# Loads of three weight matrices, one per head or half, with read descriptors over four partitions' rows, in a batched GQA decode kernel

## The chip, the cores and the metric

One core of one Trainium2 chip. The metric is the device time of one execution in microseconds (us), the median of several runs.

## The reference

```python
# B=4, one new token, D=448, 16 query heads, 8 KV heads, Sk=8192, Dh=256, bf16
xn = layernorm(A_x)
q  = xn @ A_wq                                   # (4, 16, 256)
p  = softmax(q @ k_cache.T * 256**-0.5)          # per head, over 8192 positions
s  = (p @ v_cache) @ A_wo                        # A_wo: 4096 x 448
g  = silu(mlp_block(xn))                         # small: B_w3 448 x 1792, B_w4 1792 x 448
out = A_x + s * g
# (layer norms, the unused token shift and B_w1, B_w2 left out)
```

The K and V caches are 268 MB of the 279 MB that must be read. The arithmetic is small beside that.

## The kernel before

SyncE issues all large loads on one queue. There are 32 (batch, KV head) pairs, called heads below. K and V each have two buffers of 32 KB per partition, and a load of 4 MB fills one: 128 rows of 32,768 B. `wq`, `w3` and `w4` lie in the V buffers at the start; `wo` has its own buffer.

```python
kn = sb("kn", [P, 2, NCH, DH], BF16)          # first buffer of the kernel
vb = sb("vb", [P, 2, NCH, DH], BF16)
kT = sb("kT", [P, RING, TB * P], BF16)
wo_sb = sb("wo_sb", [P, HQ, NHALF, D], BF16)
...
def prog_sp(sp):
    sp.dma_start(vflat[1][:, 0:DK * HDH], ... A_wq ...).then_inc(S["dwq"], 16)
    sp.dma_start(vflat[0][:, 0:DK * FH], ... B_w3 ...).then_inc(S["dw3"], 16)
    sp.dma_start(w4_sb..., B_w4.rearrange("(a p k) n -> p a (k n)", a=NHF, k=NFK)
                 ).then_inc(S["dw4"], 16)
    ...
    load_k(0)
    load_k(1)
    wo_src = A_wo.rearrange("(h p c) n -> p h (c n)", p=P, c=NHALF)

    def load_wo(lo, hi, sem):
        sp.dma_start(wo_sb[:, lo:hi].rearrange("p h c n -> p h (c n)"),
                     wo_src[:, lo:hi]).then_inc(S[sem], 16)

    load_wo(NLATE, HQ, "dwo")                 # heads 4..15, one load
    for h in range(2, NH):
        load_k(h)                             # waits until K buffer h % 2 is free
        load_v(h - 2)
    load_v(NH - 2)
    load_v(NH - 1)                            # in four pieces
    for i, hs in enumerate(LATE):             # heads (0, 1), (2,), (3,)
        load_wo(hs[0], hs[-1] + 1, "dwl%d" % i)
```

A partition holds, of each head of `wo`, two matrix rows that are adjacent in memory: 1,792 B. For one head the 128 partitions' pieces follow each other in memory, so 229 KB of source are contiguous, and the load takes them as 128 rows, one for each partition (the trace has 2,048 packets of 1,792 B for the 16 heads). For `w3` such a row is 12,544 B, for each half of `w4` 6,272 B.

TensorE transposes K (the lines `pst<-ident_b,kn`), multiplies with q, then multiplies the probabilities with V; VectorE and ScalarE move the transposes out of PSUM. At the end (`finish`) it works off the last heads and multiplies with `wo`.

Of the kernel before, what the change touches and what calls it, by code (L numbers as in the profile page):

```python
# [1 line left out]

# [10 lines left out]
P = 128  # L13
# [19 lines left out]
def bass_recurrent_scan__gqa_block_cached__mixer_s_mlp__decode_kernel(  # L33
# [16 lines left out]
    HQ = HD // DH  # L50
# [3 lines left out]
    NHF = 2  # L54
    DK = D * NHF // P
    assert D * NHF == DK * P and DK % 2 == 1 and D == DK * (P // 2)
    HDH, FH = HD // NHF, F // NHF
    NFK = FH // P
# [30 lines left out]
    LATE = ((0, 1), (2,), (3,))  # L89
    NLATE = sum(len(g) for g in LATE)  # L90
# [11 lines left out]
    with ExitStack() as es:  # L102
        def sb(name, shape, dty):
# [5 lines left out]
        wo_sb = sb("wo_sb", [P, HQ, NHALF, D], BF16)  # L109
# [46 lines left out]
        S = {n: es.enter_context(nc.semaphore(n)) for n in (  # L156
            ["dx", "dwq", "dw3", "dw4", "dwo", "dk0", "dk1", "dv0", "dv1", "dout"]
            + ["dvl%d" % i for i in range(NPIECE)] + ["dwl%d" % i for i in range(len(LATE))]
            + ["p_td", "p_ta", "p_sc", "p_m1", "p_m2", "p_m3", "p_tr", "p_ou", "p_pv", "p_x", "p_q", "p_h", "p_h2", "p_o"]
            + ["v_ev", "a_ev", "v_rmax", "v_diag", "v_neg", "v_ot", "a_exp", "g_q", "g_c",  # L160
               "v_s", "v_a", "v_qb", "p_qt", "v_h2", "p_hs", "v_k", "v_v", "v_po", "v_o", "g_o", "g_p", "g_f", "v_xT", "v_qT", "v_hT", "v_c", "v_w", "a_c", "v_out"])}


        vflat = [vb[:, i].rearrange("p c d -> p (c d)") for i in range(2)]
        wq_sb = vflat[1][:, 0:DK * HDH].rearrange("p (j n) -> p j n", j=DK)
        w3_sb = vflat[0][:, 0:DK * FH].rearrange("p (j n) -> p j n", j=DK)
        w4_sb = vflat[0][:, DK * FH:DK * FH + NF * D].rearrange("p (a k n) -> p a k n", a=NHF,
                                                                k=NFK)
# [16 lines left out]
        def store(eng, i):  # L185
            eng.dma_start(out2d[:, i * DQ:(i + 1) * DQ], out_b[i * PQ:i * PQ + Bn, :]
                          ).then_inc(S["dout"], 16)

        def prog_sp(sp):
            sp.dma_start(vflat[1][:, 0:DK * HDH],  # L190
                         A_wq.rearrange("d (t n) -> (d t) n", t=NHF).rearrange(
                             "(p j) n -> p (j n)", j=DK)).then_inc(S["dwq"], 16)
            sp.dma_start(vflat[0][:, 0:DK * FH],
                         B_w3.rearrange("d (t n) -> (d t) n", t=NHF).rearrange(
                             "(p j) n -> p (j n)", j=DK)).then_inc(S["dw3"], 16)
            sp.dma_start(w4_sb.rearrange("p a k n -> p a (k n)"),
                         B_w4.rearrange("(a p k) n -> p a (k n)", a=NHF, k=NFK)
                         ).then_inc(S["dw4"], 16)

            def load_k(h):  # L200
                b, g = where(h)
                if h >= 2:
                    sp.wait_ge(S["v_k"], h - 1)
                sp.dma_start(kn_dst(h), A_k_cache[b, g].rearrange("(p c) d -> p (c d)", p=P)
                             ).then_inc(S["dk%d" % (h % 2)], 16)

            def load_v(h):
                b, g = where(h)
                src = A_v_cache[b, g].rearrange("(p c) d -> p c d", p=P)
                if h < NH - 1:  # L210
                    sp.wait_ge(S["v_v"], h + 1)
                    sp.dma_start(vflat[h % 2], src.rearrange("p c d -> p (c d)")
                                 ).then_inc(S["dv%d" % (h % 2)], 16)
                else:

                    sp.wait_ge(S["v_k"], h)
                    for i in range(NPIECE):
                        lo, hi = PIECES[i], PIECES[i + 1]
                        sp.dma_start(
                            kn[:, 1 - h % 2, lo:hi, :].rearrange("p c d -> p (c d)"),  # L220
                            src[:, lo:hi, :].rearrange("p c d -> p (c d)")
                        ).then_inc(S["dvl%d" % i], 16)

            load_k(0)
            load_k(1)
            wo_src = A_wo.rearrange("(h p c) n -> p h (c n)", p=P, c=NHALF)

            def load_wo(lo, hi, sem):
                sp.dma_start(wo_sb[:, lo:hi].rearrange("p h c n -> p h (c n)"),
                             wo_src[:, lo:hi]).then_inc(S[sem], 16)  # L230

            load_wo(NLATE, HQ, "dwo")
            for h in range(2, NH):
                load_k(h)
                load_v(h - 2)
            load_v(NH - 2)
            load_v(NH - 1)
            for i, hs in enumerate(LATE):
                load_wo(hs[0], hs[-1] + 1, "dwl%d" % i)
            sp.wait_ge(S["v_out"], 1)  # L240
            store(sp, 0)
            take(sp, "dout", 16 * NDG)

        def take(eng, name, n=1):
            eng.wait_ge(S[name], n).then_inc(S[name], -n)  # L245
# [285 lines left out]
        def prog_pe(pe, xn_mark, xn2_mark):  # L531
            pe.wait_ge(S["g_c"], NPI)
            for k, (src, mark) in enumerate(((xn_b, xn_mark), (xn2_b, xn2_mark))):
                pe.wait_ge(S["v_c"], mark)
                for j in range(DK):
                    ins = pe.transpose(xT_ps[:, k, j, :],  # L536
                                       src[:, j].rearrange("b m t -> b (m t)"),
                                       ident_b[0:Bn, 0:Bn])
# [5 lines left out]
            for j in range(DK):  # L544
                for i in range(NQD):
                    ins = pe.matmul(q_ps[i * PQ:i * PQ + NHF * Bn, 0:QW],
                                    xnT[:, j].rearrange("p a b -> p (a b)"),
                                    wq_sb[:, j, i * QW:(i + 1) * QW],
                                    start=(j == 0), stop=(j == DK - 1))
# [4 lines left out]
            for k in range(NFK):  # L554
                for j in range(DK):
                    ins = pe.matmul(h_ps[:, k * NHF * Bn:(k + 1) * NHF * Bn], w3v[:, j, k, :],
                                    xn2T[:, j], start=(j == 0), stop=(j == DK - 1))
            ins.then_inc(S["p_h"], 1)
            take(pe, "v_qb")
            for m in range(QW // P):  # L560
                ins = pe.transpose(qt_ps[:, m * P:(m + 1) * P], q_b[:, m * P:(m + 1) * P],
                                   ident_b[:, :])
            ins.then_inc(S["p_qt"], 1)
            take(pe, "dw4", 16)
            take(pe, "v_hT")
            for k in range(NFK):
                for a in range(NHF):
                    i = k * NHF + a
# [5 lines left out]
            for i in range(NDG):  # L574
                ins = pe.matmul(hs_ps[i * PQ:(i + 1) * PQ, :], selb[:, :],
                                ou_f[:, i * DQ:(i + 1) * DQ], start=True, stop=True)
# [125 lines left out]

            def finish():
                f_bc(h)
                take(pe, "dwo", 16)
                pe.wait_ge(S["g_f"], 1)
                f_ou(range(NLATE, HQ - 3 * REP))
                take(pe, "v_po")
                f_warm(4)
                take(pe, "a_exp")  # L710
                pe.matmul(psm[:, P + REP:P + 2 * REP], ones_f[:, :], rowsum[:, h % 2, :],
                          start=True, stop=True)
                f_tr(ot_dst, REP).then_inc(S["p_m3"], 1)
                f_warm(2)
                take(pe, "dv%d" % ((h - 1) % 2), 16)
                f_pv(h - 1, 0, NCH)
                take(pe, "v_ot")
                f_ou(range(HQ - 3 * REP, HQ - 2 * REP))
                f_warm(2)
                take(pe, "v_po")  # L720
                f_tr(lambda dh: ot_dst(dh, 1), REP, 1).then_inc(S["p_tr"], 1)
                f_warm(3)
                take(pe, "dvl0", 16)
                pb = PIECES[NPIECE - ND]
                f_pv(h, 0, PIECES[1], pb, vl)
                take(pe, "v_ot")
                f_ou(range(HQ - 2 * REP, HQ - REP)).then_inc(S["p_ou"], 1)
                f_warm(3)
                for i in range(1, NPIECE - ND):
                    take(pe, "dvl%d" % i, 16)  # L730
                    f_pv(h, PIECES[i], PIECES[i + 1], pb, vl)
                take(pe, "v_a")
                for i in range(NDG):
                    pe.matmul(o_ps[i * PQ:(i + 1) * PQ, 0:DQ], selb[:, :],
                              ou_f[:, i * DQ:(i + 1) * DQ], start=True, stop=False)
                f_direct(NPIECE - ND)
                take(pe, "v_po")
                for dh in range(NHALF):
                    for i in range(CP):
                        pe.matmul(ol_ps[:, dh * PVW:(dh + 1) * PVW],  # L740
                                  po[:, 0, i * DH + dh:(i + 1) * DH:NHALF], sel[:, i, :],
                                  start=False, stop=False)
                f_direct(NPIECE - 1).then_inc(S["p_pv"], 1)
                take(pe, "dwl0", 16)
                f_o(LATE[0])
                take(pe, "v_ot")
                f_o(range(HQ - REP, HQ))
                for i in range(1, len(LATE)):
                    take(pe, "dwl%d" % i, 16)
                    ins = f_o(LATE[i], i == len(LATE) - 1)  # L750
                ins.then_inc(S["p_o"], 1)
# [61 lines left out]
```

## Time and profile before

| | before |
|---|---|
| median time | 657.61 us (657.61 to 658.30, 3 runs) |
| span of the profiled run | 656.9 us |
| DMA queue q1, share of 16 engines' span | 99.2% |
| TensorE busy | 85% |

These lines of the page of the kernel before say what bounds it. DMA is the busy share of the DMA engines in 40 slices of the span, in tenths; GB/s is what they moved.

```profile
DMA  8999999999999999999999999999999999999996
GB/s 360 440 413 425 434 427 437 425 439 427 437 427 435 429 435 431 431 435 427 437 429 433 429 433 429 433 429 433 429 435 431 433 431 435 429 433 433 429 425 256
DMA packets 12353, 279.13 MB, mean 425 GB/s; under 512 B 1204, under 2 KB 3256, under 8 KB 3768
...
q1 hardware_dynamic: 12328, 278.99, 99.2%
...
kn<-in_A_k_cache_dram SPq DMA_DIRECT2D x32, 4096.0 KB, 25.7
...
wo_sb<-in_A_wo_dram SPq DMA_DIRECT2D x1, 2688.0 KB, 44.3
```

The engines are at 9 tenths or more in every slice but the first and last. The third slice, where the first `wo` load runs, is at 413 GB/s, below its neighbours. A K load lands (its completion has arrived from all 16 DMA engines) 25.7 us after its issue though its bytes need 9.7 us (8 rows per engine at 1,213 ns): others stand ahead of it. The 2,052 packets between 512 B and 2 KB are the `wo` rows, and four others.

The stretch from 40 to 44 us lies inside the first `wo` load (the DMA view of the kernel before, that window):

```profile
DMA packets 855, 1.53 MB, mean 383 GB/s; under 512 B 0, under 2 KB 855, under 8 KB 855
```

The chain of waits of the kernel before, in order of time (start us, length us, what), is its last 3 us:

```profile
651.61 2.42 PE pst L687 x24
...
654.06 0.39 DVE res L526
...
654.47 0.38 DVE out_b L528
```

The 24 matmuls with the late `wo` start right after the first late `wo` load has landed on its slowest engine (651.48), so the chain runs back into the DMA stream.

The table of stretches of the kernel before; columns are stretch, length, busy us of PE, PEld, DVE, ACT and POOL with counts, granted TensorE clock, DMA share, GB/s:

```profile
620.00:624.00 4.00, 2.88 (x24) 2.70 (x25) 1.14 (x2) 0.90 (x1) 0.00 (x0) 0.62 0.99 426
624.00:628.00 4.00, 4.00 (x94) 4.00 (x92) 2.14 (x4) 3.02 (x8) 0.00 (x0) 0.95 0.97 418
```

TensorE has just begun the last head here, after a wait for its K, and the granted clock is below full for part of it. The clock records show one stretch at half clock of 3.4 us (621.0 to 624.4), and one from 651.7 us on, over the last 24 matmuls.

### The profile page before, as it was taken

What the parts mean: (1) busy time and instruction counts of PE and PEld (TensorE: products, weight loads), DVE (VectorE), ACT (ScalarE), POOL (GpSimd) and SP (SyncE); (2) the same over time, 40 slices, a digit from 0 to 9 for tenths busy, and PEclk for the clock granted to TensorE, in tenths of its full rate; (3) what the DMA queues carried; (4) which work ended last, traced back from release to release, by engine and by line L of the source; (5) the groups of instructions that cost most, each with busy time, mean ns of one, the idle gap of its engine ahead of it and who ended that gap; (6) DMA issues with size and microseconds to landing.
All of it is one profiled execution on the core that took longest, in us unless ns stands there. A gap on an engine that the chain in (4) does not pass through costs nothing. (4 is left out here: it accounts for less than half of the span.)

```text
span 656.9 us, 22864 instructions
## 1 busy us (share of the span) xinstructions
PE 556.3 (85%) x9937; PEld 476.3 (73%) x9937; DVE 276.5 (42%) x589; ACT 256.0 (39%) x364; POOL 13.4 (2%) x77
## 2 busy tenths in 40 slices
PE   1899997988888988888897888898888889888897
PEld 0487886876766887667787766798767678766775
DVE  7353554443443444434443443444334443433442
ACT  4144544442433443323444333444333344433340
POOL 2000000000000000000000000000000000000000
PEclk9698999887899878889987888988878987887998
DMA  8999999999999999999999999999999999999996
GB/s 360 440 413 425 434 427 437 425 439 427 437 427 435 429 435 431 431 435 427 437 429 433 429 433 429 433 429 433 429 435 431 433 431 435 429 433 433 429 425 256
DMA packets 12353, 279.13 MB, mean 425 GB/s; under 512 B 1204, under 2 KB 3256, under 8 KB 3768
## 3 DMA queue, kind: packets, MB, share of 16 engines
q1 hardware_dynamic: 12328, 278.99, 99.2%
q8 instruction: 7, 0.11, 0.1%
q14 instruction: 2, 0.02, 0.0%
q10 hardware_dynamic: 16, 0.01, 0.0%
HBM read 278.99 MB, written 0.00 MB: 425 GB/s over the span
## 5 line engine op out<-in xcount | busy, mean ns | idle before, releaser
L588 PE MATMUL pst<-ident_b,kn 128*128 128x128 bf16 x4096 | 347.3, 239 | 78.6 <-PEq L245 76.3
L295 ACT ACTIVATE kT<-pst 128x1024 bf16<-128x1024 bf16 x224 | 229.3, 1024 | 360.6 <-ACTq L245 359.5
L588 PEld LDWEIGHTS pst<-ident_b,kn 128*128 128x128 bf16 x4096 | 275.4, 108 | 84.3 <-issue 83.8
L293 DVE COPY kT<-pst 128x1024 bf16<-128x1024 bf16 x288 | 197.5, 691 | 263.7 <-DVEq L245 263.7
L600 PE MATMUL psc<-qc,kT 128*128 128x2 bf16 x4096 | 178.7, 165 | 0.0
L600 PEld LDWEIGHTS psc<-qc,kT 128*128 128x128 bf16 x4096 | 157.7, 98 | 28.5 <-issue 28.3
L639 PE MATMUL psv<-vb,pT 128*4 128x512 bf16 x1056 | 86.4, 378 | 0.3 <-issue 0.3
L618 PE MATMUL psm<-sel,po 128*128 128x2 f32 x272 | 36.8, 257 | 0.5 <-PEq L245 0.5
L618 PEld LDWEIGHTS psm<-sel,po 128*128 128x128 f32 x272 | 34.8, 197 | 0.9 <-issue 0.9
L639 PEld LDWEIGHTS psv<-vb,pT 128*4 128x4 bf16 x1056 | 22.3, 82 | 15.3 <-issue 0.8
L452 DVE TENSOR_REDUCE rmax<-psc 128x2 f32<-128x128 f32 x32 | 9.3, 292 | 48.8 <-DVEq L245 48.8
L470 DVE COPY po<-psv 128x512 f32<-128x512 f32 x34 | 23.5, 692 | 3.0 <-DVEq L245 2.3
L457 DVE TENSOR_REDUCE gmax<-psm 2x1 f32<-2x128 f32 x32 | 8.9, 279 | 34.7 <-DVEq L245 34.7
L317 ACT ACTIVATE pT<-psc,negb 128x64 bf16<-128x64 f32 x66 | 20.6, 331 | 5.4 <-ACTq L245 5.4
L612 PEld LDWEIGHTS psm<-diag,ones_f 2*128 2x128 f32 x66 | 14.1, 263 | 6.4 <-issue 5.4
L280 POOL COPY qc<-qT 128x4 bf16<-128x4 bf16 x32 | 5.9, 186 | 585.8 <-DVEq L469 568.6
L612 PE MATMUL psm<-diag,ones_f 2*128 2x2 f32 x66 | 16.8, 321 | 1.1 <-PEq L245 0.9
L317 ACT ACTIVATION_READ_ACCUMULATOR pT<-psc,negb 128x1 f32 x66 | 13.6, 206 | 0.0
L608 PEld LDWEIGHTS psm<-ident_f,rmax 128*2 128x2 f32 x32 | 2.6, 80 | 14.0 <-issue 14.0
L536 PE MATMUL pst<-ident_b,xn_b 4*128 4x4 bf16 x14 | 0.6, 161 | 13.6 <-DVE xn_b L365 8.9
L630 PE MATMUL psm<-rowsum,ones_f 128*128 128x2 f32 x64 | 11.6, 251 | 0.0
L536 PEld LDWEIGHTS pst<-ident_b,xn_b 4*128 4x128 bf16 x14 | 0.5, 100 | 13.6 <-issue 8.9
(101 smaller groups left out, 122.4 us busy)
## 6 DMA issues: line engine op xcount, KB each, us to landing
kn<-in_A_k_cache_dram SPq DMA_DIRECT2D x32, 4096.0 KB, 25.7
vb<-in_A_v_cache_dram SPq DMA_DIRECT2D x31, 4096.0 KB, 31.3
vb<-in_A_wq_dram SPq DMA_DIRECT2D x1, 3584.0 KB, 11.7
vb<-in_B_w_dram SPq DMA_DIRECT2D x2, 1568.0 KB, 16.6
wo_sb<-in_A_wo_dram SPq DMA_DIRECT2D x1, 2688.0 KB, 44.3
kn<-in_A_v_cache_dram SPq DMA_DIRECT2D x1, 2048.0 KB, 25.2
kn<-in_A_v_cache_dram SPq DMA_DIRECT2D x1, 1024.0 KB, 27.3
kn<-in_A_v_cache_dram SPq DMA_DIRECT2D x2, 512.0 KB, 28.5
```

The costliest lines, as they stand in the source:

```text
L293: engine.tensor_copy(dst, src).then_inc(S["v_ev"], 1)
L295: engine.activation(dst, src, ACT.Copy).then_inc(S["a_ev"], 1)
L317: ins = act.activation(pv_p[:, :, hh], sc[:, :, hh], ACT.Exp, bias=negb[:, s, hh:hh + 1], scale=SCALE, accum_out=rowsum[:, s, hh:hh + 1])
L452: v.tensor_reduce(rmax[:, :], psc[h % 2][:, 0:NCH * REP].rearrange("p (k h) -> p h k", h=REP), AX.X, ALU.max).then_inc(S["v_rmax"], 1)
L457: v.tensor_reduce(gmax[:, :], psm[0:REP, 0:P], AX.X, ALU.max).then_inc(S["v_s"], 1)
L470: v.tensor_copy(po[:, slot], psv[:, 0:CP * DH]).then_inc(S["v_po"], 1)
L588: ins = pe.transpose(dst[:, t * P:(t + 1) * P], kn[:, h % 2, GC * j + kl, half * P:(half + 1) * P], ident_b[:, :])
L600: ins = pe.matmul(psc[h % 2][:, kk * REP:(kk + 1) * REP], kT[:, j % RING, t * P:(t + 1) * P], qc[:, h % 2, half, :], start=(half == 0), st ...
L612: pe.matmul(psm[:, P:P + REP], ones_f[0:REP, :], diag[:, :], start=True, stop=True).then_inc(S["p_m2"], 1)
L618: ins = pe.matmul(dst(dh)[:, 0:width], po[:, slot, i * DH + dh:(i + 1) * DH:NHALF], sel[:, i, 0:width], start=(i == 0), stop=(i == CP - 1))
L630: pe.matmul(psm[:, P + REP:P + 2 * REP], ones_f[:, :], rowsum[:, h % 2, :], start=True, stop=True)
L639: ins = pe.matmul(psv[o:o + CP * REP, 0:CP * DH], pT[:, h % 2, kk * REP:(kk + CP) * REP], src[:, kk:kk + CP, :].rearrange("p c d -> p (c d)"),
```

## The change

The intent: rows of 1,792 B move slower than rows of 32 KB (in the trace of the kernel before 74.4 ns of stream per row in the first `wo` load, 24.1 B/ns, against packets of 1,213 to 1,221 ns, 27 B/ns). Read descriptors are here the rows of a load's source pattern, write descriptors those of its destination pattern. The source of a head is contiguous, so one read descriptor could cover four partitions' rows while the writes stay one per partition. That needs loads of one head (or one half of `w4`), since only there the rows follow each other.

```diff
+        def load_rows(eng, dst, src, rows, sem):
+            with nc.discard():
+                made = eng.dma_start(dst, src).ins
+            ap, = made.ins
+            n = ap.ap[0][1] * ap.ap[1][1]
...
+            pat = [[n // rows, rows], [1, n // rows]]
+            wide = bass.AP(ap.bass_ap.tensor, ap.bass_ap.offset, pat)
+            eng.add_instruction(copy.replace(
...
+                ins=(copy.replace(ap, ap=pat, bass_ap=wide),))).then_inc(S[sem], 16)
...
-            sp.dma_start(vflat[0][:, 0:DK * FH], ... B_w3 ...).then_inc(S["dw3"], 16)
-            sp.dma_start(w4_sb..., ... B_w4 ...).then_inc(S["dw4"], 16)
+            load_rows(sp, vflat[0][:, 0:DK * FH], ... B_w3 ..., 32, "dw3")
+            for i in range(NHF):
+                load_rows(sp, w4_sb[:, i]..., ... B_w4 ...[:, i], 32, "dw4")
...
             def load_wo(lo, hi, sem):
-                sp.dma_start(wo_sb[:, lo:hi]..., wo_src[:, lo:hi]).then_inc(S[sem], 16)
+                for hq in range(lo, hi):
+                    load_rows(sp, wo_sb[:, hq]..., wo_src[:, hq], 32, sem)
...
-            take(pe, "dw4", 16)
+            take(pe, "dw4", 16 * NHF)
...
-                take(pe, "dwo", 16)
+                take(pe, "dwo", 16 * (HQ - NLATE))
...
-                take(pe, "dwl0", 16)
+                take(pe, "dwl0", 16 * len(LATE[0]))
```

## The prediction

> **What bounds the kernel now.** The DMA engines. The page gives queue q1 99.2% of 16 engines' span; every slice but the first and last shows DMA at 9, mostly 413 to 440 GB/s. In the packet records no engine lacks a packet between about 20 and 640 us. TensorE is busy 85%; the queue's own waits (462 us for K buffers, 134 us for V buffers) leave no hole, because a 4 MB load takes 9.7 us and lands 26 to 31 us after its issue: others always stand ahead of it. Time is start + one DMA stream + a tail of about 5 us (chain of waits: 24 output matmuls, 2.42 us from 651.6, two DVE operations, the store).

> **What the change touches.** Loads of wo, w3 and w4: 6.9 of 279 MB. Packet times in the trace: 32,768 B 1213 ns; 12,544 B (w3) 469; 6,272 B (w4) 239; 1,792 B (wo) 74 at best, 79 in most of the first wo load. The slope between w4 and w3 is 27.3 B/ns, so 1,792 B would be 66 ns without overhead: each packet carries 8 to 13 ns. The first wo load (96 packets per engine) took 7.1 us on the first engine, from the landing of the second K (38.2) to its own (45.3): 74.4 ns per packet, 0.8 us over bare bytes. The late wo (32 packets) holds some 0.25 us more, w3 and w4 0.08 us each. All that can be won is about 1.2 us (0.2%).

> [...]the trace agrees that a fixed cost exists, not on which side it sits. The change cuts read descriptors to a quarter and leaves the 128 writes. If the cost belongs to the read, three quarters go: about 0.9 us. If to the write, nothing. That 1,792 B packets cost 74 ns when few engines move them and 79 when all do hints at the read side[...]. [...]

> **What it adds.** Six loads become 19, each with 16 semaphore packets of 9 ns: 13 x about 11 ns = 0.15 us per engine; and 13 more issues on SyncE, 0.33 to 0.49 us each, which run ahead: when wo is issued (3.3 us), over 30 us of loads stand before it. The third K is issued at 42.7 and the first wo load ends at 45.3 on the fastest engine, so 0.6 us less leaves no hole. The engines' instructions do not change.

> **On the critical path:** all of it; the stream is never idle. Gain 0.75 us net if the read pays; loss 0.15 us if the write pays. Weighted, about 0.5 us.

> **Prediction: 657.0 us, 656.0 to 658.3 in 8 of 10.** Faster by over 2%: 0.005; within: 0.985; slower: 0.01.

> **What would show it.** Right: the wo heads land 0.5 to 0.7 us earlier after the second K, DMA stays at 9, output matmuls start 0.5 to 1 us earlier. Write-side cost: the wo stretch stays near 380 GB/s. Issue trouble: a dip of DMA at 38 to 46 us, the third K issued after 43 us.

> **What would make it wrong.** SyncE blocked by the many issues (the last late wo already shows 10.7 us of issue) so that a K load comes late; issues over 1 us each; larger reads that slow the engines; scatter (657.61 to 658.3), as large as the gain.

The gain of 0.75 us is 0.9 us, three quarters of 1.2 us, less 0.15 us for the 13 completions; the loss is those 0.15 us alone. The 11 ns per completion are its estimate from the 9 ns that a completion's packet took in the trace.

## The result, and the profile after

| | before | after |
|---|---|---|
| median time | 657.61 us (657.41 to 658.30, 4 runs) | 657.76 us (657.51 to 658.02, 4 runs) |
| ratio after to before | | 1.0001 (95%: 0.9987 to 1.0015) |
| span of the profiled run | 656.9 us | 655.8 us |

A ratio is the mean time of one kernel's fast runs over that of the other's fast runs of the same rounds, so it is not quite the ratio of the medians. No change of the time can be seen. The interval is 0.14% or 0.9 us to either side, wider than the gain of 0.6 us that was predicted, so the time alone cannot tell whether that gain was there.

The page of the kernel after, the lines that answer to those above (`load_rows` gives one line for all 16 `wo` loads):

```profile
DMA packets 10738, 279.14 MB, mean 426 GB/s; under 512 B 1412, under 2 KB 1416, under 8 KB 2184
...
q1 hardware_dynamic: 10712, 278.99, 99.2%
...
wo_sb<-in_A_wo_dram SPq DMA_DIRECT2D x16, 224.0 KB, 35.2
```

The change did what it says: 2,048 packets of 1,792 B have become 512 of 7,168 B (the records count read descriptors: the destination's rows are as before, and the count fell to a quarter), and 208 completions of 4 B came in. But the DMA view of the kernel after, 40 to 44 us, shows no faster stretch:

```profile
DMA packets 316, 1.51 MB, mean 376 GB/s; under 512 B 106, under 2 KB 106, under 8 KB 316
```

(383 before; a packet counts where it starts, so with 7 KB packets the edge of the window is worth some per cent.)

The span of the profiled runs does differ, by 1.1 us. The chain of the kernel after says where:

```profile
650.31 1.10 PE pst L758 x8
651.41 0.39 PE pst L715 x16
651.80 1.43 PE pst L705 x24
...
653.26 0.39 DVE res L544
...
653.67 0.38 DVE out_b L546
```

The same 24 matmuls take 1.43 us here and 2.42 us before: in the profiled run of before the half-clock stretch from 651.7 us lay over them. That is 1.0 of the 1.1 us, and chance: in a second trace of the kernel before it lay elsewhere, they took 1.49 us, and the span was 655.8 us. So the spans give no gain either. The second difference is that the chain now stays on TensorE for three groups, because TensorE came late with the last head: the first late `wo` load landed at 651.12 us, and the matmuls that use it began at 651.80. The table of stretches of the kernel after:

```profile
620.00:624.00 4.00, 3.27 (x28) 3.09 (x29) 0.69 (x1) 1.02 (x1) 0.00 (x0) 0.50 1.03 442
624.00:628.00 4.00, 4.00 (x73) 4.00 (x72) 1.74 (x4) 2.57 (x6) 0.00 (x0) 0.67 0.93 401
```

The half-clock stretch at the last head's start is 6.8 us long here (619.8 to 626.6) and was 3.4 us before. From the landing of the last K to the last row maximum's transpose TensorE needs 17.26 us instead of 16.17. All four traces with the long stretch (this kernel's two, `nine_heads` and `after_256_again` below) end like this, with those matmuls 0.7 to 0.9 us after the landing; in the five with the short one it is 0.1 us.

A finer measure is needed than time or span. Each load's semaphore gets 16 increments, one per engine; their mean time is the mean landing of that load, and differences of it give the length of a stretch of the stream. From the landing records, in us:

```
                  2nd K to   3rd K to     that V to     late wo   wq to the end
                  3rd K      V of head 29 last V piece            of the stream
before            17.16      573.43       19.67         2.31      639.70
before_again      17.15      573.45       19.67         2.31      639.70
split             17.13      573.46       19.67         2.32      639.73
after             17.13      573.48       19.67         2.32      639.73
after_again       17.27      573.50       19.67         2.32      639.89
nine_heads        15.99      573.46       19.67         2.33      638.58
before_256        16.61      571.49       19.51         2.25      636.99
after_256         16.50      571.57       19.48         2.20      636.82
after_256_again   16.92      571.50       19.47         2.20      637.17
```

The first column holds the first `wo` load (96 rows per engine) and the third K (9.7 us of it), the fourth the late `wo` (32 rows). In the changed kernel neither moved: 17.13 against 17.16 us, 2.32 against 2.31. `w3` took 3.76 us before and 3.75 after. The other rows are the experiments.

### The profile page after: what moved, and what is told of

Same layout as the page of the kernel before. It is cut to its first block, busy times and chain, and to the rows that moved or that the text cites. A ratio compares the mean times of both kernels' runs of the same rounds, so it can differ in the third digit from the quotient of the medians.

```text
span 655.8 us, 22877 instructions
## 1 busy us (share of the span) xinstructions
PE 556.5 (85%) x9937; PEld 476.8 (73%) x9937; DVE 276.5 (42%) x589; ACT 256.2 (39%) x364; POOL 13.4 (2%) x77
## 3 DMA queue, kind: packets, MB, share of 16 engines
q1 hardware_dynamic: 10712, 278.99, 99.2%
## 5 line engine op out<-in xcount | busy, mean ns | idle before, releaser
L313 ACT ACTIVATE kT<-pst 128x1024 bf16<-128x1024 bf16 x224 | 229.3, 1024 | 360.9 <-ACTq L263 359.9
```

The costliest lines, as they stand in the source:

```text
L313: engine.activation(dst, src, ACT.Copy).then_inc(S["a_ev"], 1)
```

## The experiments

Theory W after the result: the fixed cost of a row sits on the write descriptor. Rival R: it sits on the read, the wide reads win, and the 13 extra completions, or the split itself, take the gain back. Rival H: a gain in the stream gets lost before the end.

### Loads alone, in six forms

A kernel that only loads, one form behind the other, eight heads' worth (1.835 MB, 64 rows of 1,792 B per engine) each:

```diff
+ # E: read 14,336 B, write 14,336 B     F: read 14,336 B, write 8 x 1,792 B
+ # G: read and write 8 x 1,792 B (E, F, G: one load, contiguous source)
+ # A: the wo rows as before, one load   B: one load per head, narrow reads
+ # C: one load per head, reads over four rows
+ ORDER = "EFGABCCBAGFE"                 # the other run: "CGBEAFFAEBGC"
```

> Loads alone, 1.835 MB each, back to back behind one 3.67 MB load; 64 rows of 1,792 B per engine, 4.21 us without overhead (27.27 B/ns). Forms: E reads and writes 14,336 B; F reads 14,336 B, writes 1,792 B; G reads and writes 1,792 B of contiguous memory, one load; A the wo rows, one load; B one load per head, narrow; C one load per head, reads widened to four rows. Theory W (the fixed cost sits on the write descriptor): E 4.27 us, F, G and A alike at 4.7 to 4.8, C within 0.05 us of B. Rival R (it sits on the read, and the extra completions took it back): F about 4.3 to 4.4 us, near E; G and A 4.7 to 4.8; C 0.3 to 0.4 us under B, and B 0.3 us or more over A. The output is wrong on purpose (x copied).

> The same forms in another order, to tell a form from its place. Both theories expect each form within 0.1 us of the run before; what each expects of the differences is as said there. The output is wrong on purpose.

Measured (difference of the landings on the slowest engine, mean of the four of each form, us): E 4.26, F 4.39, G 4.48, A 4.50, B 4.55, C 4.40. Each form's four values lie within 0.1 us. The expectation of W fell: C was 0.15 us under B, and F, G and A were not alike. Most of R's numbers fell as well: F was in its range, but G and A were 4.48 and 4.50 us instead of 4.7 to 4.8, C was 0.15 us under B instead of 0.3 to 0.4, and B only 0.05 us over A. Both sides cost something: G to F, 56 read descriptors less per engine, 0.09 us or 1.7 ns each; F to E, 56 write descriptors less, 0.13 us or 2.4 ns each. Seven more completions cost 0.05 us (B over A), 7 ns each (a later expectation works with 8). Net, the change's form was 0.10 us per 64 rows better than the kernel's, so 0.2 us could have been expected for all 128 rows. The tuned kernel showed nothing of it. And a row took 70 ns here (4.50 us / 64), while in the tuned kernel the first `wo` load took 74.4 ns per row on its first engine.

The opposite form, narrow reads with long writes, does not compile, so it was not measured.

### The split without the wide reads

```diff
-                      ... B_w3 ..., 32, "dw3")
+                      ... B_w3 ..., P, "dw3")         # likewise for w4 and wo
```

> The change without its wide reads: the same 19 loads, one read per row. Theory W: the same as the change within 0.3 us (ratio 0.9995 to 1.0010), the fourth-to-last K landing and the third K's landing within 0.1 us of the change's. Rival R: 0.5 to 0.7 us slower than the change in the stream, so the third K lands 0.5 us later and the ratio to before is 1.0010 or more.

Ratio to before 0.9999 (0.9985 to 1.0012), median 657.78 us, 5 runs. The stream equals that of the change in every column (17.13, 2.32). So R is out in the tuned kernel: there is no gain of the wide reads for the split to take back, and in this trace the split costs the stream 0.03 us. The DMA view of this kernel, 40 to 44 us:

```profile
DMA packets 962, 1.53 MB, mean 383 GB/s; under 512 B 107, under 2 KB 962, under 8 KB 962
```

107 completions inside the window, and the rate is that of the kernel before.

### Three heads of wo less

```diff
-            load_wo(NLATE, HQ, "dwo")
+            load_wo(NLATE, NLATE + NLD, "dwo")   # NLD = 9; three heads use other heads' weights
```

> The kernel before, with the first wo load cut from 12 heads to 9 (three heads' matmuls read other heads' weights: wrong on purpose). 0.69 MB less, 24 packets per engine of 74.4 ns: 1.79 us less in the stream. If the stream reaches the end one to one, as theories W and R both hold, the time falls by 1.6 to 1.9 us (ratio 0.9971 to 0.9977). Rival H (a gain in the stream is lost to a hole before the third K or in the last matmuls): under 1 us.

Ratio 0.998 (0.9966 to 0.9993), median 656.82 against 658.07 us. The stream lost 1.17 us up to the third K, not 1.79: about 0.6 us was lost at the third K, whose issue (42.47 us) waits until its buffer is free. Of its first 16 packets, 12 took 1.6 to 2.2 us, where in the kernel before none took more than 1.25. The rest reached the end of the stream (1.12 us) and the time. This is between the theories: a gain of the stream does reach the time, but only so far ahead of the third K. The prediction had held that 0.6 us would leave no hole; a saving of 1.8 us is beyond what fits there. This trace also has the long half-clock stretch, so that TensorE was 0.9 us late at its end.

### The same loads beside working engines

```diff
+ pe:  290 matmuls of 512 columns out of SBUF
+ v:   90 copies of 128 x 1024 bf16 in SBUF
+ act: 60 copies of 128 x 1024 bf16 in SBUF
```

> The same loads in the order of the first such run (E F G A B C C B A G F E), with TensorE, VectorE and ScalarE working out of SBUF and PSUM beside them. In the tuned kernel a 1,792 B packet took 79 ns in the middle of the wo load and 74.4 ns of stream per row; alone it took 74 and 70. If the engines' work causes that, A rises here from 4.50 to about 4.75 us and its packets to 79 ns; and if that part sits on the write, F rises as A does and C stays 0.15 us under B. If the engines' work is not the cause, all forms stay within 0.05 us of the run without it. The output is wrong on purpose.

No effect: packets of 1,792 B stayed at 74 ns (median and mean), the second half gave C 4.42, B 4.50, A 4.52, G 4.57, F 4.34, E 4.25. VectorE ended its copies at 43 us, when the second half had hardly begun. In the first half, where all three engines worked, one DMA engine lost 1.4 us in G; the mean landings, which this moves little, gave A 4.55 and C 4.43 there, far from the 4.75 expected of A if the engines were the cause. So the 4 ns per row that the tuned kernel pays over the loads alone do not come from work of this kind on the compute engines.

### Shorter rows

```diff
+ SIZES = dict(E=(7168, 7168), F=(7168, 896), G=(896, 896),     # (read, write) in bf16 elements
+              a=(7168, 256), b=(256, 256), c=(7168, 512), d=(512, 512))
```

> One load of 1.835 MB each from contiguous memory: reads of 14,336 B or of the write's size, writes of 14,336, 1,792, 1,024 and 512 B. The first two runs gave 1.7 ns per read descriptor and 2.4 ns per write descriptor. Linear in the count, 1,024 B (112 per engine): narrow 4.69, wide read 4.51 us; 512 B (224 per engine): narrow 5.13, wide read 4.76 us. If the cost of a read descriptor cannot be hidden behind a short write any more, the 512 B narrow load takes over 5.5 us and wide reads win over 10% there. The output is wrong on purpose.

Means of two, except F and G: 512 B narrow 5.21, wide 4.74; 1,024 B narrow 4.71, wide 4.46; 1,792 B narrow 4.45, wide 4.44; 14,336 B 4.25. Linear in the count as expected, within 0.1 us. Wide reads win 9% at 512 B, 5% at 1,024 B, 0 to 2% at 1,792 B (the two earlier runs gave 2%). At 512 B that is 2.2 ns per read descriptor and 2.3 per write descriptor (0.47 and 0.49 us over 216), and the narrow load ran at 352 GB/s where 14,336 B rows ran at 432.

### The traces once more

> The kernel before once more, for its trace: the third K should land 16.8 to 17.0 us after the second on the slowest engine, as in the first trace (16.87). This tells how far a difference of 0.1 us can be trusted.

> The changed kernel once more. From the loads alone: 128 wo rows per engine of which 96 reads fall away at 3 ns each, 13 more completions at 8 ns each, so 0.2 us less in the stream: ratio 0.999 to 1.001, and the third K 16.70 to 16.85 us after the second on the slowest engine (16.77 in the first trace).

The kernel before nearly repeated itself: 16.78 us on the slowest engine, just outside what was expected, and every column of the table within 0.02 us. The changed kernel gave ratio 1.0002 (0.9988 to 1.0016), median 657.91 us, and 17.04 us on the slowest engine, outside what was expected. The third K was issued 1.1 us later than in its first trace (43.42 against 42.36), seven of its first 16 packets took 1.5 to 2.0 us instead of 1.1 to 1.3, and the mean of the stretch is 0.14 us longer. So the first column holds the lateness of the third K too, and differences of 0.1 us in it need a second trace. Still, 0.2 us of gain, expected from the loads alone, is not there in either trace, nor in the late `wo` (2.32 us in both).

### A different start in SBUF

What differed between the loads alone and the tuned kernel? The addresses: in the tuned kernel `kn` starts at byte 16,512 of each partition and `wo_sb` at 163,968, both 128 modulo 256; in the loads alone the six forms' destinations started at 0 modulo 256 (these are the addresses in the built programs; the traces do not show them). No other start was tried, and no run shows why the start should matter. Theory M: it does, every write pays for it, and a write that is slower than its read hides whatever the read saves. Its 4 ns per row are an estimate, the 74.4 ns of the tuned kernel less the 70.3 ns of the loads alone (4.50 us over 64 rows).

```diff
+        pad = es.enter_context(nc.sbuf_tensor("pad", [P, 64], BF16))   # 128 B
         t = [...]                                                      # the destinations
```

> The loads alone in the first order (E F G A B C C B A G F E), with every destination moved by 128 B: in the tuned kernel wo_sb, kn and vb start at 128 modulo 256 bytes in a partition, in the first loads-alone runs the destinations started at 0 modulo 256. Theory M [...]: every 1,792 B write costs about 4 ns more, so A, F, G and B rise by 0.26 us (A to 4.76, F to 4.65), E by under 0.05, and C comes within 0.05 us of B. If the start does not matter, all forms stay within 0.05 us of the run without the shift. The output is wrong on purpose.

Measured, in us: E 4.30, F 4.79, G 4.82, A 4.82, B 4.82, C 4.82 (means of two). A, B and C, the kernel's form, the split and the change, are now equal to 0.01 us. A row costs 75.3 ns, 5.0 ns more than before the shift. The rise is larger than the 4 ns that M expected, the most in F (4.39 to 4.79, where 4.65 was expected). The DMA view shows it; first the run with destinations at 0 modulo 256, three windows of 3 us inside A, B and C:

```profile
DMA packets 685, 1.22 MB, mean 407 GB/s; under 512 B 4, under 2 KB 685, under 8 KB 685
...
DMA packets 756, 1.21 MB, mean 403 GB/s; under 512 B 84, under 2 KB 755, under 8 KB 756
...
DMA packets 265, 1.26 MB, mean 421 GB/s; under 512 B 89, under 2 KB 89, under 8 KB 265
```

Then the run with destinations at 128 modulo 256, windows inside the same forms:

```profile
DMA packets 639, 1.14 MB, mean 381 GB/s; under 512 B 2, under 2 KB 639, under 8 KB 639
...
DMA packets 712, 1.16 MB, mean 387 GB/s; under 512 B 80, under 2 KB 707, under 8 KB 712
...
DMA packets 238, 1.14 MB, mean 380 GB/s; under 512 B 79, under 2 KB 79, under 8 KB 238
```

With 0, C stands out at 421 GB/s. With 128, all three are near the 383 GB/s of the tuned kernel, and the wide reads have nothing left to win. The median record of a 1,792 B packet is 79 ns with the shift and 74 without: the 79 ns of the tuned kernel, which the prediction took for a sign of the read side, were the sign of this.

### The pad in the tuned kernels

```diff
+        pad = sb("pad", [P, 64], BF16)
         kn = sb("kn", [P, 2, NCH, DH], BF16)
```

> The kernel before, with a 128 B pad ahead of the first buffer, so that kn, vb and wo_sb start at multiples of 256 B. Theory M: 4 ns less per packet of wo, 0.5 us over its 128 rows per engine (wo to the third K: 17.16 us before, about 16.75 here, mean over engines; late wo 2.31 before, 2.18 here). If every K and V packet saves 4 ns too, 2 us more, ratio 0.996; if only the short rows do, ratio 0.999 to 1.000.

> The changed kernel with the same pad. Theory M: now the wide reads show: 0.15 us less than the padded kernel before in the first wo load (mean over engines from second to third K), 0.05 us less in the late wo; in the time, no difference that the runs can tell from the padded kernel before (within 0.1%). If wide reads never pay in this kernel, the stretch is the same within 0.05 us.

The kernel before with the pad: 655.21 us against 658.13, ratio 0.9962 (0.9948 to 0.9975), 5 runs. It beats both kernels, by 128 bytes of unused space. The stream is 2.71 us shorter: 1.94 us of it in the 59 loads of K and V between the third K and the V of head 29, 472 packets per engine, 4.1 ns each; 0.55 us in the first `wo` stretch; 0.16 in the last V pieces; 0.07 in the late `wo`. Its DMA view, 40 to 44 us:

```profile
DMA packets 910, 1.63 MB, mean 408 GB/s; under 512 B 0, under 2 KB 910, under 8 KB 910
```

and that of the changed kernel with the pad:

```profile
DMA packets 351, 1.67 MB, mean 418 GB/s; under 512 B 118, under 2 KB 118, under 8 KB 351
```

These two are 408 and 418 GB/s where the kernels without the pad had 383 and 376. With the pad, the wide reads do show, near what was expected: 0.11 us less up to the third K (16.50 against 16.61) and 0.05 us in the late `wo`. The second came back in another trace (2.20 us both times); the first did not (16.92, with a late third K), so it rests on one trace. But the time of the changed kernel with the pad was 656.95 us, ratio 0.9984 (0.9971 to 0.9998), with one run at 654.90 and four from 656.65 to 657.11.

> The changed kernel with the pad once more: its five times were 654.9 once and 656.65 to 657.11 four times, though its stream ended 0.17 us earlier than the padded kernel before's. Theory T: the upper times come from the end on TensorE, where a stretch at half clock of 6.8 us instead of 3.4 us falls into the last head (as in both traces of the changed kernel, where the last row maximum came 17.25 us after the last K instead of 16.15). Then a trace at about 655 us shows a short stretch and one at about 657 us a long one, the last late wo landing at 649.8 plus or minus 0.3 us in both. Rival: the wide reads themselves cost it; then a slow trace shows the last late wo landing 1.5 us or more later.

Six runs: 654.51, 654.86, 655.03, 656.09, 656.40 and 657.64 us, ratio 0.9966 (0.9953 to 0.9979). So the kernel has a spread of 2 to 3 us of its own, and its upper values are not a cost of each execution. This trace (span 654.5 us, a time of 656.40) has the long half-clock stretch of 6.8 us, and the last row maximum came 17.09 us after the last K, against 16.26 in the trace at 654.90 us; so far T. But its last late `wo` also landed 1.05 us later on the slowest engine (650.86 against 649.81; 0.35 us in the mean), outside T's range: from the second to the third K it took 0.42 us longer, with the third K issued at 42.35 instead of 41.98 us. Neither theory has it whole. The wide reads did not cost it in the late `wo`, which took 2.20 us in both traces. Whether they change the time of the padded kernel at all, these runs cannot tell: the intervals of the three sets overlap.

## Why the prediction was right or wrong

- **The bound: right, but not to the last microsecond.** The stream is never idle, and 2.71 us less in the stream were about 2.5 us less in the time (ratio 0.9962 of 658 us). Where the half-clock stretch is long, as in both traces of the changed kernel, TensorE ends 0.7 to 0.9 us behind the data. Its last head still starts when the last K lands, so a gain ahead of that K should show in the time, but a gain in the late `wo` should not; no run separates the two.
- **The size and range: right**, 657.76 us inside 656.0 to 658.3, within 2%. The whole cost in dispute was about 1.2 us, so any split of it had to land near there: the range held both a gain of 0.75 us and a loss of 0.15 us, and falling inside it says nothing for the mechanism. That a loss of 0.15 us gives the measured median exactly is luck, since the stream grew by 0.03 us in one trace and 0.19 in the other. The best guess, 0.5 us faster, leaned to the read side, and no trace shows that gain.
- **"Gain 0.75 us net if the read pays; loss 0.15 us if the write pays": nearer the second, and both sides pay.** The gain was worth 0 here, and the sign named for a write-side cost came: the `wo` stretch stayed near 380 GB/s (376). With rows that start at 128 modulo 256 bytes in the destination a row took 75.3 ns whether its read was narrow or wide (A, B and C equal at 4.82 us, F at 4.79), as if the write set the pace and the read's cost ran beside it. Without that start a read saved was worth 3.1 ns (C against B, 0.15 us over 48 reads), a third of the 8 to 13 ns that the prediction put on a packet.
- **"13 x about 11 ns = 0.15 us per engine": too much for this kernel.** Completions cost 7 ns each in the loads alone with destinations at 0 modulo 256 (B over A, 0.05 us for seven), and nothing that shows with destinations at 128 (B and A both 4.82 us); in the tuned kernel the split alone added 0.03 us to the stream, about 2 ns for each of the 13.
- **"hints at the read side": wrong.** This was the step that failed. (Nor were few engines at work where packets took 74 ns: by 39.4 us all but one were on the `wo` rows, and the median rose to 79 only after 40.4.) In the loads alone, the 79 ns come when the destinations are moved by 128 B, and in the tuned kernel they go when the pad moves the buffers by 128 B: with it the 1,792 B packets took 74 ns at the median and in nine of ten.
- **"so 0.6 us less leaves no hole": right in one trace, with little to spare.** With the pad the kernel before had its `wo` 0.5 us earlier, and the first packets of the third K took no longer than 1.31 us. 1.79 us less lost about 0.6 us there, and in the second trace of the changed kernel a late issue (43.42 us) was enough to slow seven packets.
- **SyncE's issues:** they did no harm. The 12 `wo` issues took 14.9 us from 4.2 us on, long before the third K (42.36 us).

Left open: why the first 2 us of the `wo` load in the tuned kernel show 74 ns packets although they start at the same offset (in the kernel before, the rise came about when the last engine joined, at 40.4 us; nothing tests whether that is the reason), and what decides whether the half-clock stretch at the last head is 3.4 or 6.8 us long.
